# Pooled attention and a four-expert MLP on one core: a batch's keys in two loads, attention pieces at other places of the product loop, and weight sums earlier

## The chip, the cores and the metric

The kernel runs on one core of a Trainium2 chip. The metric is the device time of one execution in microseconds (us). Six executions of the kernel before took 502.47 to 507.32 us, the median is 502.71 us. A core has five engines with a queue of instructions each: TensorE (PE, matrix products), VectorE (DVE), ScalarE (ACT), GpSimd (POOL) and SyncE (SP). Every queue is worked off in order. Semaphores tie the queues together. Transfers are issued from GpSimd's and SP's queues here, and some from ScalarE's at the end.

## The reference

Attention with pooled keys and values over 8 batches of 8 heads (576 tokens, 64 elements a head), and then four experts, weighted by normalised domain probabilities, over all 4608 tokens:

```
k_p = k.reshape(B, H, 72, 8, 64).mean(axis=3)      # 8 rows of keys become one
v_p = v.reshape(B, H, 72, 8, 64).mean(axis=3)
attn = softmax(q @ k_p^T / 8)                       # 576 x 72 for each head
x = (attn @ v_p), heads side by side                # 4608 x 512
p = domain_probs / (domain_probs.sum(-1) + 1e-9)
for e in range(4):
    out += p[:, e] * (relu(x @ w1[e]) @ w2[e])      # 512 -> 1024 -> 512
```

## The kernel before, in words

**Chunks.** The tokens are worked off in nine chunks of 512. Chunk b, for b from 0 to 7, holds the first 512 tokens of batch b. The 64 tokens that each batch leaves over (the remainder) make chunk 8. For each chunk and each expert there is an up product (x times w1, then relu, into `H`) and a down product (`H` times w2, times the probability, added into `acc`).

**Seven products instead of eight.** From chunk 1 on, every up and every down product is split into 2 by 2 blocks, and seven block products of sums and differences take the place of eight (Strassen's scheme in Winograd's form). The sums need VectorE: `weight_sums` and `first_weight_sums` make them once for each expert's w2 and w1 (three into `wt_bf` or `wu_bf`, a fourth in place into the weights, 0.68 to 0.69 us each), `hidden_sums` makes four for each chunk and expert (`S3`, `S2`, two in `H`), `x_sum` four for each chunk (three into `xs`, one in place into `xT`).

**The product loop.** The loop over `g` runs through 7 times 32 steps, and one more. A turn of it is called a slot here; slot g has step i = g mod 7 of chunk-and-expert pair t = g div 7. Chunk c fills slots 28(c-1) to 28(c-1)+27. A slot issues, in this order: a hidden sum (steps 0, 2, 3), the up product's step for one half of the hidden units (unit 0: 4 matmuls), the up step one slot behind for unit 1 (4 matmuls), a hidden sum (step 1), the down product's step one slot behind of the pair before (8 matmuls), then the attention pieces of this slot and the weight sums of this slot. ScalarE takes the steps 0, 1, 2, 3 and 5 of an up product out of PSUM, VectorE the steps 4 and 6 (`relu_sum`, L533). Step 6 and the copy of step 0 (ScalarE, L565) use the same bank: the copy of the next pair waits for the `relu_sum` before, and the next step 1 of TensorE for the copy. VectorE adds the down products into `acc` (L695), except that for expert 0 ScalarE writes the first of each place (L693), and that one step in seven is taken out by ScalarE into `addend` and added by GpSimd (L634, the pooled add). When a chunk's last expert is done, `store` writes `acc` out from SP's queue, and the next chunk's first write of that place waits for the store.

**Attention.** Pieces for a batch: `load_part` (keys and values in four loads of two rows of the eight, the second to fourth adding in the transfer onto the first), `load_q`, `load_q_rem`; `fold_keys` and `fold_values` (VectorE adds the two rows that are left: two `kp` of 0.41 us, one `vp` of 0.41); `queries`, `keys` and `turn` (transposes, from batch 2 on by transfers from SP's queue: `qT`, `kpT`, `xT`); `scores` for each of four pairs of heads (TensorE, then exp on ScalarE, 1.02 us); `context` for each of four rows of tokens (TensorE, then a reciprocal of 0.20 us and a division of 0.69 us on VectorE, `x_tok`); then the four `x_sum`. Every second batch also has the remainder of two batches: `rem_queries`, `rem_scores`, `rem_context`, `rem_turn`. From batch 2 on scores and contexts use one pair of PSUM banks, `att`. Batches 0 and 1 are folded from eight whole rows (`load_whole`, into the room of `wt_bf`) and transposed on TensorE; batch 0 stands ahead of everything, batch 1 in `first_chunk`, which works chunk 0.

**What sets the order.** All five engines are under a manual schedule: each engine's instructions stand in the order in which the Python code emits them. `pieces_later` is a table, written by hand, from slots to attention pieces; the attention of batch b (2 to 7) is put into the slots of chunk b-1, and a few of its pieces sooner. `sums` maps slots to weight sums. Loads from GpSimd's queue stand in the same queue as the pooled adds.

**The places that the change touches.** `load_part` (L113 to L120), the weight sums in `first_chunk` (L730, L746) and in the dictionary `sums` (L874), the table in `pieces_later` (L796 to L829), and the loads of batch 2 ahead of `first_chunk`:

```
        load_w2(3)
        load_part(2, 0)
        load_part(2, 1)
        load_q(2)
        load_part(2, 2)
```

## Time and profile before

| What | before |
|---|---|
| median of six executions | 502.71 us |
| lowest, highest | 502.47, 507.32 us |
| the profiled execution | 507.32 us |
| its span | 505.5 us |
| mean granted TensorE clock | 0.986 |
| busy: TensorE, VectorE, ScalarE, GpSimd | 98%, 74%, 60%, 24% |
| start of slot 0 of the product loop | 76.62 us |
| start of slots 28, 56, 84, 112, 140, 168, 196, 224 | 130.31, 182.74, 236.37, 288.99, 342.12, 393.80, 443.64, 492.55 us |

The profile is of one execution, the slowest of the six. Times in it count from the start of its span. A window's line gives, for a stretch of time, its length, the busy time of each engine with the number of its instructions, the granted clock, the mean share of the 16 transfer engines and the rate. A timeline's line gives start, duration, engine, line of the kernel, operation, output and input; in brackets stands how long the engine had been idle before it, and what ended that idle time. A group that follows without a break is put together on one line (x8). Starts of slots are the starts of the first matmul of the up step of unit 0, found by counting matmuls.

### The profile page before, as it was taken

The numbers are of one execution on the slowest core, as the hardware profiler recorded it, in microseconds if no ns is written. First come the engines' busy times: TensorE is split into PE (matmuls) and PEld (weight loads), VectorE is DVE, ScalarE is ACT, GpSimd is POOL, SyncE is SP. The second block draws the span as 40 slices with busy tenths as digits, with TensorE's granted clock in tenths as the row PEclk, the third lists the DMA queues.
The fourth block names the chain that finished last, engine by engine and source line by source line (L and its number), as shares of the span: only waits on it lengthen the run. The fifth ranks groups of instructions, "written<-read, shape, count | busy, mean of one in ns | idle before, by whom it ended". The sixth has DMA issues, their size and how long they took to land.

```text
span 505.5 us, 11342 instructions
## 1 busy us (share of the span) xinstructions
PE 494.1 (98%) x4613; PEld 410.8 (81%) x4622; DVE 372.2 (74%) x741; ACT 302.3 (60%) x561; POOL 119.3 (24%) x113
## 2 busy tenths in 40 slices
PE   7999999999999999999999999999999999999996
PEld 4766558878888987988788878888888888888885
DVE  3363779989866897778677868887688757876774
ACT  3366624775568557655766576656855576556650
POOL 7230062423344235102441145001101110111010
PEclk9599999999999999999999999999999999999999
DMA  9999999698669849921798179730210010004003
GB/s 161 212 209 203 198 82 112 106 91 66 85 107 98 86 65 111 132 54 21 72 152 80 25 71 134 66 66 22 84 34 1 22 64 1 12 23 84 1 0 84
DMA packets 104611, 41.70 MB, mean 82 GB/s; under 512 B 77664, under 2 KB 103008, under 8 KB 104560
## 3 DMA queue, kind: packets, MB, share of 16 engines
q0 software_dynamic: 60256, 22.69, 42.2%
q1 hardware_dynamic: 43728, 17.77, 18.6%
q8 instruction: 36, 0.59, 0.5%
q10 hardware_dynamic: 576, 0.52, 0.3%
q14 instruction: 15, 0.12, 0.1%
HBM read 45.69 MB, written 9.44 MB: 109 GB/s over the span
## 4 chain that ended last, share of the span: by engine, by line
PE 82%; DVE 8%; DMA 5%; issue 2%; ACT 2%; POOL 0%; DVEq 0%; ACTq 0%; POOLq 0%
PE o_ps L620 34%; PE unit L552 33%; PE unit L479 5%; DVE acc L695 3%; DMA xT<-x_tok 2%; PE o_ps L646 2%; PE att L311 1%; DMA q_sb<-in_q_dram 1%; DMA out_dram<-acc 1%; PE unit L678 1%; DVE H L533 1%; PE att L337 1%; DVE S L189 1%; PE unit L242 1%; DVE x_tok L326 1%
## 5 line engine op out<-in xcount | busy, mean ns | idle before, releaser
L695 DVE SCALAR_TENSOR_TENSOR acc<-o_ps,p_all,acc 128x256 f32<-128x256 f32 (+1 forms) x285 | 127.0, 486 | 59.8 <-PE o_ps L620 40.2
L620 PEld LDWEIGHTS <-H 128*128 128x128 bf16 x1320 | 129.1, 98 | 17.0 <-issue 1.2
L552 PEld LDWEIGHTS <-w_bf 128*128 128x128 bf16 x1024 | 98.0, 98 | 15.7 <-issue 4.2
L533 DVE CUSTOM_DVE_ANT_0 H<-unit,partial 128x512 bf16<-128x512 f32 x128 | 87.6, 686 | 24.4 <-PE unit L552 16.1
L620 PE MATMUL o_ps<-w_bf,H 128*128 128x256 bf16 x792 | 102.6, 273 | 0.4 <-ACT o_ps L628 0.2
L552 PE MATMUL unit<-xT,w_bf 128*128 128x256 bf16 x672 | 96.3, 273 | 0.9 <-ACT unit L565 0.9
L634 POOL TENSOR_TENSOR acc<-acc,addend 128x512 f32<-128x512 f32 x24 | 32.5, 1354 | 274.3 <-ACT addend L632 240.2
L567 ACT COPY partial<-unit 128x512 f32<-128x512 f32 x128 | 72.0, 590 | 33.5 <-PE unit L552 32.9
L552 PEld LDWEIGHTS <-wu_bf 128*128 128x128 bf16 x768 | 73.1, 98 | 10.7 <-issue 2.3
L552 PE MATMUL unit<-xs,wu_bf 128*128 128x256 bf16 x512 | 76.9, 273 | 0.0
L620 PE MATMUL o_ps<-wt_bf,H 128*128 128x256 bf16 x528 | 68.4, 273 | 0.0
L620 PEld LDWEIGHTS <-S 128*128 128x128 bf16 x528 | 51.6, 98 | 7.4 <-issue 1.0
L569 ACT ACTIVATE H<-unit 128x512 bf16<-128x512 f32 x64 | 38.8, 606 | 28.0 <-PE unit L552 28.0
L573 ACT ACTIVATE H<-unit 128x512 bf16<-128x512 f32 x64 | 38.1, 596 | 26.2 <-PE unit L552 25.8
L565 ACT COPY unit<-unit 128x512 f32<-128x512 f32 x64 | 37.3, 583 | 24.4 <-PE unit L552 19.8
L118 POOL DMA_DIRECT2D kraw<-in_k_dram x18 | 25.2, 1398 | 58.4 <-DMA kraw<-in_k_dram 58.4
L552 PE MATMUL unit<-xs,w_bf 128*128 128x256 bf16 x256 | 38.5, 273 | 0.0
L693 ACT ACTIVATE acc<-o_ps,p_all 128x256 f32<-128x256 f32 x72 | 30.2, 471 | 13.6 <-PE o_ps L620 10.6
L620 PE MATMUL o_ps<-w_bf,S 128*128 128x256 bf16 x264 | 34.2, 273 | 0.6 <-DVE acc L695 0.4
L620 PE MATMUL o_ps<-wt_bf,S 128*128 128x256 bf16 x264 | 34.2, 273 | 0.0
L552 PE MATMUL unit<-xT,wu_bf 128*128 128x256 bf16 x224 | 33.7, 273 | 0.0
L315 ACT ACTIVATE expT<-att 72x1024 bf16<-72x1024 f32 x26 | 26.5, 1020 | 7.1 <-PE att L311 7.1
(129 smaller groups left out, 523.7 us busy)
## 6 DMA issues: line engine op xcount, KB each, us to landing
out_dram<-acc SPq DMA_DIRECT2D x32, 256.0 KB, 3.4
w_bf<-in_moe_w_dram POOLq DMA_DIRECT2D x7, 1024.0 KB, 23.4
q_sb<-in_q_dram POOLq DMA_DIRECT2D x7, 512.0 KB, 10.8
kraw<-in_k_dram POOLq DMA_DIRECT2D x24, 144.0 KB, 5.6
vraw<-in_v_dram POOLq DMA_DIRECT2D x24, 144.0 KB, 6.7
w_bf<-in_moe_w_dram POOLq DMA_DIRECT2D x2, 512.0 KB, 11.8
wt_bf<-in_k_dram POOLq DMA_DIRECT2D x2, 288.0 KB, 5.5
wt_bf<-in_v_dram POOLq DMA_DIRECT2D x2, 288.0 KB, 8.8
```

The source lines that it names most:

```text
L315: nc.scalar.activation(out=expT[:, 2 * pair:2 * pair + 2].rearrange("j h a b t -> j b (h a) t"), in_=sc_ps[0:SP].rearrange("j b h (a t) -> ...
L479: nc.tensor.matmul(out_ps, lhsT=w1_bf[:, e, kc, fc * P:(fc + 1) * P], rhs=xT[:, kc, at], start=(kc == 0), stop=(kc == KC - 1), skip_group_ ...
L533: nc.vector._custom_dve(TENSOR_ADD_SAT, out=dst, in0=ps, in1=part, s0=LARGEST, s1=0.0)
L552: nc.tensor.matmul(ps[:, n * HN:(n + 1) * HN], lhsT=lhs[:, kc, f:f + P], rhs=rhs[:, kc, :], start=(not grows and n == 0 and kc == 0), stop ...
L565: nc.scalar.copy(out=units[unit][1][:], in_=ps)
L567: nc.scalar.copy(out=part[:, step - 2], in_=ps)
L569: nc.scalar.activation(out=quarter(0, 0), in_=ps, func=ACT.Relu)
L573: nc.scalar.activation(out=quarter(0, 1), in_=ps, func=ACT.Relu)
L620: nc.tensor.matmul(ps[:, j], lhsT=lhs[:, i, j * P:(j + 1) * P], rhs=rhs[:, i, :], start=(not grows and i == 0 and j == 0), stop=(i == HF - 1),
L634: nc.gpsimd.tensor_add(out=dst, in0=dst, in1=addend[:])
L693: nc.scalar.activation(out=dst, in_=o_ps, func=ACT.Copy, scale=prob)
L695: nc.vector.scalar_tensor_tensor(out=dst, in0=o_ps, scalar=prob, in1=dst, op0=ALU.mult, op1=ALU.add,)
```

## The change

It has four parts.

1. Batch 2's keys: rows 0 to 5 of each eight are loaded in one transfer into the room of expert 2's `wt_bf`, rows 6 and 7 in another into `raw_k`. No key transfer of this batch adds any more; VectorE adds the pieces, `fold_wide(0)` in slot 1 (two adds of 72x1024), `fold_wide(1)` in slot 5 (one). Keys and values now have loads of their own. All loads of batch 2 move from before `first_chunk` to a place inside it, behind `fold_values(1)`.
2. The first three w1 sums of expert 2 move from slots 3, 5 and 6 into the second pass of the first chunk; those of expert 3 from slots 9, 9 and 10 to behind `keys(1)`. The fourth sums go to slots 7 and 13 (from 9 and 13). The last w2 sum of expert 1 goes from slot 9 to slot 8.
3. The pieces of batches 2 to 7 get other slots. Batch 2: keys folded in slot 5 (from 9), values in 12 (from 10), scores in 11, 12, 15, 17 (from 13 to 16), contexts in 18, 19, 21, 22 (from 17, 18, 20, 21), x sums in 25, 26, 26, 26 (from 24, 25, 25, 26). Others: queries and keys six slots ahead of the chunk, scores at -1, 3, 5, 6, contexts at 8, 11, 14, 18, x sums at 21, 22, 25, 26.
4. The loads of the following batch stand at other slots; the queries' load is in the second slot of a chunk from batch 4 on (from the eighteenth).

The arithmetic is the same but for the order of batch 2's key additions. The diff:

```diff
-    def load_part(b, part):
-        for src, raw in ((k, raw_k), (v, raw_v)):
-            rows = src[b].rearrange("h (j r) d -> j h r d", r=POOL)[:, :, 2 * part:2 * part + 2, :]
-            if part:
-                nc.gpsimd.dma_start(out=raw[:], in_=rows, accum_op=ALU.add)
-            else:
-                nc.gpsimd.dma_start(out=raw[:], in_=rows)
+    def rows_of(src, b, lo, hi):
+        return src[b].rearrange("h (j r) d -> j h r d", r=POOL)[:, :, lo:hi, :]
+
+    def load_part(b, what, part):
+        src, raw = ((k, raw_k), (v, raw_v))[what]
+        nc.gpsimd.dma_start(out=raw[:], in_=rows_of(src, b, 2 * part, 2 * part + 2),
+                            accum_op=ALU.add if part else ALU.bypass)
+
+    wide_k = wt_bf[0:SP, 2].rearrange("j s i d -> j (s i d)").rearrange(
+        "j (h r d) -> j h r d", h=H, r=POOL - 2)
+
+    def load_wide(part):
+        if part == 0:
+            nc.gpsimd.dma_start(out=wide_k, in_=rows_of(k, BUSY, 0, POOL - 2))
+        else:
+            nc.gpsimd.dma_start(out=raw_k[:], in_=rows_of(k, BUSY, POOL - 2, POOL))
...
+    def fold_wide(part):
+        a, b, c = (wide_k[:, :, 2 * i:2 * i + 2, :] for i in range(3))
+        if part == 0:
+            nc.vector.tensor_add(out=a, in0=a, in1=b)
+            nc.vector.tensor_add(out=a, in0=a, in1=c)
+        else:
+            nc.vector.tensor_add(out=raw_k[:], in0=raw_k[:], in1=a)
...
-        sums = {e: first_weight_sums(e) for e in range(2)}
+        sums = {e: first_weight_sums(e) for e in range(E)}
...
                     sums[1][i - 4]()
+                    if i < 7:
+                        sums[2][i - 4]()
...
         keys(1, every)
+        each(*sums[3][0:3])
...
         fold_values(1, every)
+        load_wide(0)
+        load_q(2)
+        load_wide(1)
+        load_part(2, 1, 0)
+        load_q_rem(0)
+        load_q_rem(1)
+        for part in range(1, NR):
+            load_part(2, 1, part)
         down_plain(0, 1, 0)
...
-        for b in range(2, B + 1):
-            start = 7 * E * (b - 2)
+        usual = dict(
+            queries=-6, keys=-6, values=-2, scores=(-1, 3, 5, 6), contexts=(8, 11, 14, 18),
+            q=1, k=(-2, 0, 3, 6), v=(-2, 0, 3, 6), x=(21, 22, 25, 26), rem=(-3, 17, 21, 22),
+        )
+        plans = {b: usual for b in range(BUSY, B + 1)}
+        plans[BUSY] = dict(
+            queries=1, keys=5, values=12, scores=(11, 12, 15, 17), contexts=(18, 19, 21, 22),
+            q=9, k=(7, 10, 13, 16), v=(13, 16, 24, 27), x=(25, 26, 26, 26), rem=(2, 6, 8, 9),
+        )
+        plans[B] = dict(usual, x=(25, 25, 26, 26))
+        plans[BUSY + 1] = dict(usual, values=4, v=(5, 8, 11, 14))
...
+            if b == BUSY:
+                put(start + 1, lambda: fold_wide(0))
+                put(start + 5, lambda: load_q_rem(BUSY), lambda: fold_wide(1))
             if b < B:
-                q_at, k_at, scores_at, contexts_at, loads_at = (
-                    (1, 9, (13, 14, 15, 16), (17, 18, 20, 21), (11, 12, 14, 25, 28)) if b == 2
-                    else (0, 3, (10, 11, 12, 13), (15, 16, 18, 20), (5, 6, 8, 11, 14)) if b == 3
-                    else (-4, -4, (3, 4, 5, 6), (8, 9, 11, 13), (-2, 17, 0, 3, 6)))
...
-                put(start + (6 if b == 2 else -3), lambda i=i: rem_queries(i))
-                put(start + (10 if b == 2 else 16), lambda i=i: rem_scores(i))
-                put(start + (12 if b == 2 else 18), lambda i=i: rem_context(i))
-                put(start + (13 if b == 2 else 19), lambda i=i: rem_turn(i))
-            for n, slot in enumerate((24, 25, 25, 26) if b == 2 else (24, 24, 25, 26) if b == 3
-                                     else (16, 16, 20, 23) if b < B
-                                     else (23, 24, 24, 25)):
-                put(start + slot, lambda b=b, n=n: x_sum(b, n))
...
-        load_part(2, 0)
-        load_part(2, 1)
-        load_q(2)
-        load_part(2, 2)
-        load_q_rem(0)
-        load_q_rem(1)
         first_chunk()
...
-        for at, pieces in (((4, 2), weight_sums(3)[2:]), ((3, 5, 6, 9), first_weight_sums(2)), ((9,), weight_sums(1)[3:]), ((14, 14, 16, 16), weight_sums(2)),
-                           ((9, 9, 10, 13), first_weight_sums(3))):
+        for at, pieces in (((4, 2), weight_sums(3)[2:]), ((7,), first_weight_sums(2)[3:]), ((8,), weight_sums(1)[3:]), ((14, 14, 16, 16), weight_sums(2)),
+                           ((13,), first_weight_sums(3)[3:])):
```

## The prediction

> **What bounds the kernel now.** I read the page first: TensorE is busy 98% of the span, so time is won only where TensorE waits. Then I cut the product loop into its chunks of 28 slots (a slot is one turn of the loop, 16 matmuls of 128x256) by windows; the edges are the starts of slots 0, 28, 56 and so on in the timeline.
>
> ```profile
> core 0: us, PE busy (x) PEld busy (x) DVE busy (x) ACT busy (x) POOL busy (x), PEclk, DMA share, GB/s
> 76.62:130.31 53.69, 53.34 (x524) 45.10 (x524) 48.59 (x98) 34.05 (x63) 15.84 (x14) 1.00 0.92 97
> 130.31:182.74 52.43, 51.99 (x498) 44.99 (x496) 41.42 (x86) 33.47 (x62) 18.11 (x16) 1.00 0.77 88
> 182.74:236.37 53.63, 53.08 (x531) 45.43 (x528) 42.96 (x85) 34.52 (x63) 15.41 (x14) 1.00 0.68 81
> 236.37:288.99 52.62, 52.00 (x498) 44.98 (x496) 40.33 (x81) 33.32 (x62) 15.38 (x14) 1.00 0.75 81
> 288.99:342.12 53.13, 52.93 (x530) 45.45 (x528) 42.71 (x83) 34.42 (x63) 15.42 (x14) 1.00 0.73 80
> 342.12:393.80 51.68, 51.68 (x498) 44.98 (x496) 39.36 (x78) 33.53 (x62) 3.81 (x4) 1.00 0.13 35
> 443.64:492.55 48.91, 48.91 (x451) 43.82 (x449) 34.62 (x66) 29.63 (x58) 4.54 (x5) 1.00 0.12 28
> ```
>
> The granted clock is 1.00 in all of them. The last line has no attention: 28 slots in 48.91, so 1.75 a slot. The sixth holds one batch's attention and no wait: 2.77 more, which is four score pieces of 0.43 and four context pieces of 0.26. The remainder pieces of every second batch add 0.90 (slot 72 with scores, slot 74 with context), and slot 0 has 0.41 of the plain product. So chunks 1 to 5 should take 52.99, 51.68, 52.58, 51.68 and 52.58. They take 0.70, 0.75, 1.05, 0.94 and 0.55 more: 3.99 us is all that the loop can give back. The timeline says who is late:
>
> ```profile
> 113.81 0.42 PE L337 MATMUL att<-vp,expT 72*128 72x65 bf16 x8 [0.20 <-DVE x_tok L326]
> ...
> 127.45 0.43 DVE L189 TENSOR_TENSOR xs<-xT 128x512 bf16<-128x512 bf16 x1 [1.30 <-DMA xT<-x_tok]
> ...
> 131.28 0.68 DVE L533 CUSTOM_DVE_ANT_0 H<-unit,partial 128x512 bf16<-128x512 f32 x1
> 132.04 0.57 ACT L565 COPY unit<-unit 128x512 f32<-128x512 f32 x1 [1.80 <-DVE H L533]
> 132.66 0.70 PE L552 MATMUL unit<-xT,w_bf 128*128 128x256 bf16 x5 [0.44 <-ACT unit L565]
> ...
> 185.08 0.38 PE L552 MATMUL unit<-xT,w_bf 128*128 128x256 bf16 x2 [0.43 <-ACT unit L565]
> ...
> 260.25 0.84 ACT L693 ACTIVATE acc<-o_ps,p_all 128x256 f32<-128x256 f32 x2 [2.38 <-DMA out_dram<-acc]
> ...
> 303.50 2.50 DVE L189 TENSOR_TENSOR S<-H 128x1024 bf16<-128x1024 bf16 x1
> 303.61 1.83 POOL L634 TENSOR_TENSOR acc<-acc,addend 128x512 f32<-128x512 f32 x1
> ```
>
> In chunk 1 VectorE's queue is late (slot 9 loses 0.24, 16 loses 0.09, 18 loses 0.40: slot lengths against 1.75 plus their pieces). At slots 28 and 30 (0.75) VectorE first waits 1.30 for the last transpose of x; so `relu_sum` ends at 131.95, ScalarE's copy (L565) waits for it, and TensorE for the copy. Slots 56 and 58 (0.74) show the same chain behind crowded slots 52 to 54. Slot 72 loses 0.28 to ScalarE's copy L628. Slot 96 loses 0.42 to a store that lands late, 103 loses 0.52 to a transposed x that lands 1.43 late, and 121 loses 0.53 where a VectorE sum stands still beside GpSimd's add.
>
> **The change, part by part.** Every number below is of the profiled execution: 507.32, its span 505.5 and 1.8 around it. It is 4.61 above the median of the six, 502.71. I take the loop's waits to be alike in the others and put the sum on the median.
>
> *Weight sums sooner.* Six of 0.69 leave slots 3, 5, 6, 9, 9 and 10. Slots 7 to 10 held 2.32, 0.68, 4.25 and 1.78 of VectorE work (4.25 is `H` 0.69, two `kp` of 0.41, `w1_bf` and `w2_bf` 0.68 each, two `wu_bf` of 0.69) in 7.86 of TensorE; now they hold 3.00, 2.26, 0.69 and 0.68. Three sums go into the second pass of the first chunk. Two fall in idle stretches of 2 to 3 us. The third follows the sum at 50.76 to 51.44 and ends at 52.04 (operations overlap by 0.09), where the next add started at 51.62. The queue then has no gap up to the `qT` copies, so these start 0.32 later, at 55.98 and 56.31; TensorE, which wrote the two banks again at 56.20 and 56.45, waits: cost 0.32 (ends 0, if the 0.6 of other work shifts, and 0.6, the whole sum). The other three stand after the `kpT` copy, before an idle of 2.92 (60.76 to 63.68); fold of values ends near 62.6. They cost nothing; were that cover gone, 1.9.
>
> *Keys of batch 2.* GpSimd's four key loads become two, and two accumulating issues of 1.39 go. VectorE gets three adds of about 0.69 (the fold of 72x1024 took 0.686): two in slot 1, one in slot 5. Counting from slot 0, S2 ends at 80.96, the two adds at 82.2; slot 1's list is late by 0.6, slot 3 lost 0.69, so the queue is level by slot 4. Cost 0. All loads of batch 2 now stand on GpSimd's queue behind the fold of batch 1's values, at about 63. Before, the second part was issued at 64.92, so only bytes of the first parts come later. In the transfers between 60 and 130 us a 512 KB `q_sb` took 8.8 to land and the 144 KB parts 6.1 and 6.8, so the six rows (432 KB by size) should land before 72; VectorE wants them at 80.9. The four value parts wait for each other: issued near 66, 74, 80 and 86, the last issue ends near 88; GpSimd's pooled add of slot 5 wants to start at 89. Cost 0, ends 0 and 0.53 (the price of 121, if the chain is later). On SP's queue `qTr` moves to slot 2, `kpT` to 6, `x_rem` to 9, each behind stores; their inputs are there and their readers stand four slots or more behind: 0.
>
> *Attention of batch 2.* Contexts at 18, 19, 21, 22. Chunk 1's 0.70 goes. I added VectorE's queue slot by slot, each operation at the later of its input and its predecessor's end; by this sum the division of slot 17 ends 2.01 after the start of slot 18 before (the trace: 113.76, 2.06). After, the division of slot 21 ends 1.85 into slot 22, TensorE wants the bank at 1.75: 0.15 back. On SP's queue the transpose of batch 3's queries (issue 3.21 at 123.87) is now ahead of x's last transpose, and keys' transpose behind both. From slot 22: division 1.85, first x transpose 1.2, `qT` 2.0 to 3.2, x 2.4 to 5 from issue to landing (113.82 to 116.19, 122.33 to 127.30): 7.7 to 11. The sum that reads x comes at 8.2; five queue entries (2.6) later `relu_sum` must be done 0.65 before slot 29, at 12.3: nothing is lost up to a landing at 9.7. Keys land at 9.1 to 12, scores of slot 27 want them at 10.8. I take 0.2, ends 0 and 1.3, for the 0.75 that goes.
>
> *Later batches.* Scores, contexts and x sums stand further apart; slots 52 to 54 drop from 6.88 to 5.22 of VectorE work, and x's last transposition has 4.7 us before its reader with queries' load already over. So 0.74 (56, 58) and 0.52 (103) go. The heaviest new slot, 77, holds 3.63 in 2.23; by the same queue sum adds end at most 1.46 after a slot's end, and the banks allow 1.95. Cost 0.
>
> *What it leaves.* 96 and 121 have one root: GpSimd's pooled add stands in its queue behind a value part (L118) which waits for the part before; the add starts 2.1 to 3.5 after the slot. After the change the order there is the same, with the query load put in front. ScalarE's 72 has the same list. I count half of 0.42, 0.53 and 0.28 as gone: 0.62 (ends 0 and 1.23).
>
> The rows for that are `S` 2.50 against 0.68 and the add's 1.83 against 1.27. [...]
>
> Sum: gone 0.70 + 0.75 + 0.74 + 0.52 + 0.62 = 3.33; new 0.32 + 0.15 + 0.2 + 0.1 = 0.77. Net 2.56: 502.71 - 2.56 = **500.1**.
>
> **Rivals.** *A: all waits go.* 3.99 less the 0.32 that is sure: 499.0. For it: no queue sum passes its limit. Against: GpSimd's order at the late adds stays. *B: the waits move.* The three half-terms stay (0.62 back) and SP's order at slot 22 costs 1.0 instead of 0.2: 500.1 + 1.4 = 501.5. For it: the transposes at 119.51 and 122.33 landed 6.2 and 5.0 later with key and value parts in flight. Against: only one part is in flight there. *C: the six rows come late.* In-order VectorE stands at slot 1 until they land. L109 loads took 23.6 and 21.9 to land at 20 to 50 us, behind weights: 63.1 + 23.6 = 86.7, against 82.3 (80.96 and 1.3 of slack): 4.4 lost, 504.5, slower than before; it decides from a landing at 84.9 on. Against: weights have landed by then, since the first part landed by 64.9.
>
> **How the numbers follow.** Forecast 0.51, A 0.18, B 0.24, C 0.07. About 0.5% (2.5 us) is what a measurement here tells from no change, so 500.2 is the border and the forecast lies on it: 0.6 of the forecast, all of A and little of B are faster, 0.50 in all; slower than 505.2 is the far part of C and what I don't see, 0.06; 0.44 between. Range: A's bound and 0.3 below, B with the upper ends of its terms above: 498.7 to 502.2; C and half of the unseen lie outside.
>
> **What would show it.** Right: chunks near 53.1, 51.9, 52.7, 52.0, 52.9; no wait of `xs` on `xT` at slots 25 and 105; TensorE idle 0.3 before the `qT` transposes at 56. Wrong: VectorE idle before L213-like adds of 72x1024 at slot 1, TensorE waiting on `kpT` in slot 27, GpSimd's add of slot 5 past 91, or stores that hold ScalarE at the first expert of each chunk.

## The result, and the profile after

The changed kernel is slower. Its median is 508.27 us over 32 executions (503.16 to 514.15), that of the kernel before 503.16 us over 69 on the same chips. The ratio is 1.0072, with a 95% interval of 1.0053 to 1.0091; it is taken over the undisturbed executions alone, the medians over all. The forecast was 500.1, with a range that ended at 502.2.

The two profiled executions, 509.63 us (span 507.8) and 507.32, can't be compared by their totals. The one before had 13.7 us at half clock (a granted clock of 0.50) ahead of the loop and started slot 0 at 76.62; the one after started it at 72.67. A measure that leaves this out is the time from the start of slot 0 to the start of slot 196: 367.02 us before, 373.27 after, 6.25 more. It is called the loop's length below.

The windows of the changed kernel, cut at slots 0, 28, 56 and so on as before (columns: from:to, length, busy time and instructions of TensorE, its weight loads, VectorE, ScalarE and GpSimd, granted clock, share of the transfer engines, GB/s):

```profile
72.67:134.14 61.47, 56.42 (x529) 46.10 (x528) 50.34 (x100) 34.98 (x63) 17.94 (x16) 0.94 0.81 85
134.14:185.81 51.67, 51.67 (x498) 44.99 (x496) 40.52 (x83) 33.50 (x62) 16.85 (x15) 1.00 0.69 85
185.81:239.48 53.67, 52.93 (x530) 45.43 (x529) 43.18 (x84) 34.47 (x63) 15.54 (x14) 1.00 0.61 79
239.48:292.24 52.76, 52.01 (x499) 44.99 (x497) 42.40 (x82) 33.48 (x62) 15.50 (x14) 1.00 0.65 81
292.24:344.84 52.60, 52.60 (x530) 45.47 (x529) 41.84 (x84) 34.35 (x63) 15.55 (x14) 1.00 0.63 81
344.84:396.10 51.26, 51.26 (x494) 44.96 (x493) 39.24 (x78) 33.50 (x62) 3.39 (x4) 1.00 0.13 35
```

The forecast named 53.1, 51.9, 52.7, 52.0 and 52.9 for the first five. Chunks 2 and 5 are there, chunks 3 and 4 are 1.0 and 0.8 over, and chunk 1 is 8.4 over, with a granted clock of 0.94. Of the 8.4, 0.43 is no loss: the new table puts the first score piece of batch 3 into slot 27, and the forecast had not moved it. (Chunk 6 is shorter by as much, 51.26 instead of 51.68.) TensorE's timeline shows where in chunk 1 (start, duration, engine, line, operation, in brackets the idle time before it and what ended it):

```profile
94.94 1.04 PE L638 MATMUL o_ps<-wt_bf,H 128*128 128x256 bf16 x8
100.27 0.61 PE L329 MATMUL att<-qT,kpT 64*128 64x256 bf16 x4 [4.29 <-DMA kpT<-kp]
...
102.49 1.92 PE L638 MATMUL o_ps<-w_bf,S 128*128 128x256 bf16 x8
104.33 0.61 PE L329 MATMUL att<-qT,kpT 64*128 64x256 bf16 x4
```

Before the first scores of batch 2, in slot 11, TensorE waits 4.29 us for the transpose of the keys. Behind it, eight matmuls that took 1.04 take 1.92: the clock has fallen. Three windows around it:

```profile
97.00:100.00 3.00, 0.00 (x0) 0.00 (x0) 0.00 (x0) 0.00 (x0) 0.00 (x0) 0.83 0.90 130
100.00:103.00 3.00, 2.73 (x15) 1.72 (x16) 0.17 (x1) 1.56 (x2) 0.00 (x0) 0.50 1.62 111
103.00:106.00 3.00, 3.00 (x18) 1.67 (x17) 1.79 (x5) 1.02 (x1) 1.40 (x1) 0.53 0.03 2
```

In the first no engine works at all, and the clock falls in it, at 98.96; in the next two it is 0.50 and 0.53. In all 6.8 us were at half clock, by which slots 12 and 13 lost 1.89 and 0.44. (The loss of a slot is its length less 1.75 and less the time of its attention pieces. The expectations below have some numbers that are up to 0.05 higher.) What the wait was for: the same transpose, from issue to landing, in the kernel before and in the changed kernel.

```profile
95.05 1.21 SPq L229 DMA_TRANSPOSE kpT<-kp  x1
102.76 0.39 PE L311 MATMUL att<-qT,kpT 64*128 64x256 bf16 x4
DMA to landing us min/median/max: 4.6/4.6/4.6
```

```profile
DMA to landing us min/median/max: 11.4/11.4/11.4
```

Before, nobody on TensorE waited for it: it landed at 99.66 and was read by the scores at 102.76. After, it was issued at 88.86 and landed at 100.22. Since the two loops start 3.95 apart, the times are better counted from the start of slot 0: it was issued 2.2 sooner (16.2 instead of 18.4) and landed 4.5 later (27.6 instead of 23.0), while its first reader stood 2.8 sooner (ready at 95.97, so 23.3 instead of 26.1). SP's queue and GpSimd's queue of the changed kernel at that time:

```profile
86.43 2.38 SPq L721 DMA_DIRECT2D out_dram<-acc  x2
88.86 1.25 SPq L247 DMA_TRANSPOSE kpT<-kp  x1
90.43 0.38 SPq L721 DMA_DIRECT2D out_dram<-acc  x1
92.47 1.67 SPq L418 DMA_TRANSPOSE x_rem<-x_tok  x1
```

```profile
84.68 1.72 POOL L652 TENSOR_TENSOR acc<-acc,addend 128x512 f32<-128x512 f32 x1
85.95 1.11 POOL L154 DMA_DIRECT2D q_rem<-in_q_dram  x1
87.33 0.86 POOL L119 DMA_DIRECT2D kraw<-in_k_dram  x1 [0.28 <-DVE kp L241]
88.18 0.92 POOL L139 DMA_DIRECT2D q_sb<-in_q_dram  x1
89.07 0.71 POOL L154 DMA_DIRECT2D q_rem<-in_q_dram  x1
```

Two stores of 256 KB stand ahead of the transpose on its own queue, and the 512 KB load of batch 3's queries (`q_sb`) is issued 0.7 ahead of it on the other. The stores also hold up the issue. The pooled keys were done at 87.03, but the second store was issued only at 88.44, when VectorE's add into `acc` had ended (88.42), and the transpose behind it. In the kernel before it was issued at once when the pooled keys were done (95.02).

The other three losses are of one kind, a VectorE sum beside GpSimd's pooled add. VectorE at the two `kp` sums and at slot 65, with the add of slot 65:

```profile
84.90 2.13 DVE L241 TENSOR_TENSOR kp<-kraw 72x512 bf16<-72x512 bf16 x2
...
199.91 3.03 DVE L199 TENSOR_TENSOR S<-H 128x1024 bf16<-128x1024 bf16 x1
200.56 1.82 POOL L652 TENSOR_TENSOR acc<-acc,addend 128x512 f32<-128x512 f32 x1
```

The two `kp` sums take 2.13 instead of 0.8 and cost 0.85 in slot 7 (84.68 to 86.40 is the add). `S` takes 3.03 instead of 0.68 and costs 1.06 in slot 65; slot 93 loses 1.07 the same way.

So the loop's losses are 4.57 in slot 11, 2.33 in slots 12 and 13, 0.85, 1.06 and 1.07 by the sums, and 0.30 in slots 16 and 22: some 10.2, against the 3.99 that it lost before. The difference, 6.2, is that of the loop's lengths.

### The profile page after: what moved, and what is told of

Its sections match the earlier page's. It is cut to its first block, busy times and chain, and to the rows that moved or that the text cites. A ratio compares the mean times of both kernels' runs of the same rounds, so it can differ in the third digit from the quotient of the medians.

```text
span 507.8 us, 11350 instructions
## 1 busy us (share of the span) xinstructions
PE 492.0 (97%) x4613; PEld 408.1 (80%) x4622; DVE 378.4 (75%) x744; ACT 303.3 (60%) x561; POOL 115.9 (23%) x111
## 4 chain that ended last, share of the span: by engine, by line
PE 85%; DVE 8%; DMA 4%; issue 1%; ACT 0%; POOL 0%; SPq 0%; DVEq 0%; ACTq 0%; POOLq 0%
PE o_ps L638 37%; PE unit L570 36%; PE unit L497 4%; DVE acc L713 2%; DMA kpT<-kp 2%; DMA wt_bf<-in_v_dram 2%; PE att L329 2%; DVE S L199 1%; PE o_ps L664 1%; PE att L355 1%; PE unit L696 1%; DVE wt_bf L199 1%; DVE kp L241 1%; DVE H L551 1%; DVE x_tok L344 0%
## 5 line engine op out<-in xcount | busy, mean ns | idle before, releaser
L551 DVE CUSTOM_DVE_ANT_0 H<-unit,partial 128x512 bf16<-128x512 f32 x128 | 87.8, 686 | 31.1 <-PE unit L570 26.1
L587 ACT ACTIVATE H<-unit 128x512 bf16<-128x512 f32 x64 | 38.7, 605 | 27.3 <-PE unit L570 27.3
L119 POOL DMA_DIRECT2D vraw<-in_v_dram x24 | 31.6, 1315 | 36.3 <-DMA vraw<-in_v_dram 24.3
```

What stands on the lines that cost most here:

```text
L119: nc.gpsimd.dma_start(out=raw[:], in_=rows_of(src, b, 2 * part, 2 * part + 2), accum_op=ALU.add if part else ALU.bypass)
L551: nc.vector._custom_dve(TENSOR_ADD_SAT, out=dst, in0=ps, in1=part, s0=LARGEST, s1=0.0)
L587: nc.scalar.activation(out=quarter(0, 0), in_=ps, func=ACT.Relu)
```

## The experiments

Each is a short edit of the changed kernel unless it is said otherwise. The loop's length stands beside the median where it tells more. A trace is of one execution, and the executions of a kernel differ by several us, so a wait is read from the trace and the whole time from the median.

### The query load later (e1)

```diff
-            q=9, k=(7, 10, 13, 16), v=(13, 16, 24, 27),
+            q=14, k=(7, 10, 13, 16), v=(13, 16, 24, 27),
```

> The changed kernel with one number altered: the load of batch 3's queries stands at slot 14 of the loop instead of slot 9, behind all key loads and the first value load of batch 3 on GpSimd's queue. Theory T1 (the 512 KB query load, which GpSimd issued at 88.18 us, 0.7 us ahead of the transpose of batch 2's keys, shares the transfers' bandwidth with it and so stretches it from 2.6-4.4 to 11.1 us): the keys' transpose lands within 5 us of its issue, TensorE's wait of 4.29 before the first scores of slot 11 falls to 0-0.5, the stretch at half clock behind it goes too, and the time falls by 6 to 7 us against the changed kernel, to about 501.5. Rival T2 (the transpose is slow because of the place to which the change moved it, among the stores of the slots 6 to 8 and the key load, whatever the queries do): it still takes over 8 us, TensorE waits over 2, and the time stays within 2 us of the changed kernel's.

Measured: median 504.01, ratio to before 0.9983 (0.9944 to 1.0022); loop 368.32. The transpose took 7.7 us, between what the two theories said:

```profile
98.56 0.39 PE L329 MATMUL att<-qT,kpT 64*128 64x256 bf16 x4 [1.55 <-DMA kpT<-kp]
```

The wait falls to 1.55 and the clock stays at 1.00 from 96 to 106. So the query load is a part of it, not all. Other losses stood in this execution: a wait of 0.58 for the remainder's queries in slot 6, 0.52 in slot 9, 0.60 in slot 27, 0.39 in slots 28 and 30, and 1.10 in slot 93 for an `S` beside the pooled add.

### Work for TensorE while it would wait (e2)

```diff
+        if b == BUSY and pair == 0:
+            for _ in range(20):
+                open_bank(bank[:, 0])
```

> The changed kernel with 20 matmuls of 128x512 added ahead of the first scores of batch 2 (slot 11). They write the bank that the scores then write again, so nothing of their result is used: they only keep TensorE at work while it would wait for the keys' transpose. By the matmuls of 128x256 (1.75 us for 16) 20 of them take about 4.4 us, as long as the wait of 4.29. Theory T3 (the half clock from about 99 to 106 us is a consequence of that wait): the granted clock stays 1.00 through slots 11 to 13, and the time is about 2.4 us less than the changed kernel's although work was added (slots 12 and 13 lost 1.93 and 0.48). Rival T4 (the half clock comes of something else, as the work done before): the clock falls all the same and the time is equal to the changed kernel's or up to 4.4 more.

Measured: median 506.73, ratio 1.0052 (1.0013 to 1.0090), 1.5 under the changed kernel's median where 2.4 were expected. In the profiled execution the transpose took 8.5 and landed at 97.62, so the wait would have been 2.2 only (TensorE's other work was done at 95.45); TensorE was busy throughout and the clock stayed at 1.00. By itself this does not settle what the half clock comes of. The holds below do.

### The pooled add ahead of the value load (e3)

```diff
-            q=1, k=(-2, 0, 3, 6), v=(-2, 0, 3, 6),
+            q=1, k=(-2, 0, 5, 8), v=(-2, 0, 5, 8),
```

> The changed kernel with the third key and value loads of batches 5 to 8 at slot 5 instead of 3 of their chunks, and the fourth at 8 instead of 6, so that on GpSimd's queue the pooled add of each chunk stands ahead of the third value load, which waits for the second to land. Theory T5 (slots 65 and 93 lose 1.10 each because the add is late and so runs beside VectorE's S sum, which grows from 0.68 to 3.03): the S sums of slots 65 and 93 take about 0.7, the two losses go, and the time falls by about 2.2 us against the changed kernel. Rival T6 (the add would meet another VectorE sum wherever it stands, or the later parts make the keys of those batches late): the time stays within 0.7 us, and another operation with two inputs takes over 1.5 beside the add.

Measured: median 507.48, ratio 1.0049 (1.0007 to 1.0091); loop 370.76, 2.5 shorter than the changed kernel's. GpSimd's add and VectorE's `S` of slot 65:

```profile
197.14 1.26 POOL L652 TENSOR_TENSOR acc<-acc,addend 128x512 f32<-128x512 f32 x1 [3.23 <-ACT addend L650]
198.36 1.41 POOL L119 DMA_DIRECT2D kraw<-in_k_dram  x1
```

```profile
199.08 0.68 DVE L199 TENSOR_TENSOR S<-H 128x1024 bf16<-128x1024 bf16 x1
```

The add stands ahead of the load, is over before `S`, and both have their plain lengths; slots 65 and 93 lose nothing. T5 holds in the trace, and not by chance: with this edit the three adds of slots 62, 90 and 118 all take 1.26, while in the traces of the changed kernel, of e1, e2 and e4 the adds of these places take 1.82 to 1.84, in the changed kernel beside hidden sums of 3.03, 3.04 and 1.58. The third of these sums is not the first of a pair's (`S` from `H`) but the second (`S` from `H` and `S`), and TensorE does not wait in that chunk (52.60 busy of 52.60). The median can't tell it, since the wait of slot 11 (4.46 here) and the half clock behind it are still there, and the executions of this kernel differ by several us (502.31 to 513.82).

### The last key rows sooner (e4)

```diff
-                put(start + 5, lambda: load_q_rem(BUSY), lambda: fold_wide(1))
+                put(start + 3, lambda: fold_wide(1))
+                put(start + 5, lambda: load_q_rem(BUSY))
```

> The changed kernel with the last add of batch 2's wide key rows at slot 3 instead of 5, so that the pooled keys of batch 2 are summed before GpSimd's pooled add of chunk 1 begins. Theory T7 (slot 7 loses 0.89 because the sum of the pooled keys took 1.80 beside that add): the sums take about 0.4 each, slot 7 is level, and the time falls by about 0.9 us; the keys' transpose is issued no earlier than its slot, so the wait of slot 11 stays at 3 to 4.5. Rival (the time that the queue gains at slot 7 only makes the wait at slot 11 longer, since that ends with the transpose, whatever comes before): no change of the whole, with the wait 0.9 longer.

Measured: median 506.94, ratio 1.0029 (0.9986 to 1.0073). The two `kp` sums:

```profile
84.64 0.75 DVE L241 TENSOR_TENSOR kp<-kraw 72x512 bf16<-72x512 bf16 x2
```

Slot 7 is level, as T7 said, but the edit is not what did it: the add began at 86.51 here, 1.8 later than in the changed kernel and after the `kp` sums, which stand where they stood. In e1 and e2, without this edit, the add was as late and slot 7 as level. So T7 is not tested by this run; e7 and e8, where the sums come two slots sooner and end ahead of the add, are what supports it. The add ran beside an `S` of 2.22 at 86.69, which held nobody up. In slot 6 TensorE waited 0.72 for the transpose of the remainder's queries, as it did for some time in e1 and e2. The wait of slot 11 was 1.94, less than expected (no fall of the clock followed): GpSimd's queue was 1.8 later here (the remainder's load at 87.72 instead of 85.95), so that the key part was still under way, and the query load behind it, when the store ahead of the transpose had landed. The table in the next section has these times.

### The keys ahead of the stores (e7)

```diff
-            queries=1, keys=5, values=12,
+            queries=1, keys=3, values=12,
```

with `fold_wide(1)` in slot 3 as above.

> The changed kernel with the keys of batch 2 two slots sooner: the last add of its wide rows and the two sums of the pooled keys at slot 3 instead of 5, so that the transpose stands at slot 4 of SP's queue, ahead of the stores of slots 5 and 6 instead of behind them. The query load of batch 3 stays at slot 9. Theory T8 (stores and transposes on SP's queue land in the order of their issue: 90.07, 92.83, 100.22, 101.90, 102.58 in the changed kernel; so the transpose first waits for the store in front of it, 4.0 us, and then shares its time with the query load of GpSimd's queue, 7.4 us): the transpose is issued near 83 and lands by 88, TensorE does not wait for it at slot 11, no half clock follows, and the time falls by 6 to 7 us, to about 501.5. Rival T9 (VectorE, with 1.5 us of sums more in slot 4, is late with the hidden sums and TensorE loses it there): the wait of slot 11 goes, but slots 5 and 6 lose 0.5 to 1.5 us, and the time is 502.5 or more.

Measured: median 502.68, ratio 0.9974 (0.9935 to 1.0013), 5.6 under the changed kernel; loop 364.70, 8.6 shorter than it. The transpose:

```profile
DMA to landing us min/median/max: 5.0/5.0/5.0
```

No wait in slot 11, no half clock in the loop; slot 5 loses 0.17, so T9's price is small. The query load stood where the change put it. What it loses besides is above all `S` in slot 65 (1.11). The median is 1.2 above the 501.5 expected, and the ratio does not tell the kernel from the one before; against the changed kernel the gain is clear.

### Three corrections together (e8)

The last edit, the query load at 14, and the loads at 5 and 8.

> The changed kernel with three corrections together: the keys of batch 2 two slots sooner as in e7, the query load of batch 3 at slot 14 instead of 9 as in e1, and the third and fourth key and value loads of batches 5 to 8 at slots 5 and 8 as in e3. If the causes are those named so far, the three are worth the wait of 4.29, the half clock of 2.4, the 0.89 of slot 7 and the twice 1.10 of slots 65 and 93: 9.8 us less than the changed kernel's profiled execution, and about 499 to 500 as a median, below both kernels. Rival: other waits take their place (the transposes and loads of batch 3 come closer to their readers with the queries at slot 14), and the time stays at 501.5 to 503.

Measured: median 501.37, ratio 0.9959 (0.9923 to 0.9995): faster than the kernel before. The transpose took 2.7 us. The windows, cut as above:

```profile
72.30:126.21 53.91, 53.82 (x529) 45.05 (x528) 48.43 (x98) 34.61 (x63) 17.89 (x16) 1.00 0.76 95
126.21:178.37 52.16, 51.99 (x499) 45.02 (x497) 41.92 (x85) 33.68 (x62) 16.93 (x15) 1.00 0.70 84
178.37:230.98 52.61, 52.61 (x531) 45.46 (x529) 41.09 (x84) 34.49 (x63) 15.46 (x14) 1.00 0.64 81
230.98:282.66 51.68, 51.68 (x499) 44.97 (x497) 40.28 (x82) 33.51 (x62) 15.42 (x14) 1.00 0.66 82
282.66:335.27 52.61, 52.61 (x531) 45.48 (x529) 41.09 (x84) 34.49 (x63) 15.45 (x14) 1.00 0.65 81
```

TensorE is busy in all of these five chunks but 0.26 us. The loop takes 364.06, 9.2 less than the changed kernel's. The median is 1.4 over the 499 to 500 expected; six of its twelve executions took 499.2 to 501.3, and the others, up to 505.8, have no profile.

### The scores later (e9)

```diff
-            scores=(11, 12, 15, 17),
+            scores=(13, 14, 15, 17),
```

> The changed kernel with the first two score pieces of batch 2 at slots 13 and 14 instead of 11 and 12, so that 3.5 us more of products stand before the first reader of the keys' transpose; loads, stores and transposes stay as they are. Theory T8 with T3: the transpose still takes 8 to 11.4 us, TensorE waits 0 to 0.9 for it at slot 13, and since no long wait is left, the clock stays at 1.00; the time falls by 5.5 to 7 us against the changed kernel. Rival T4 (the half clock has another cause than the wait): it still falls to half near 99 to 106 us, and the time falls by only 3.5 to 4.3.

Measured: median 506.60, ratio 1.0025 (0.9992 to 1.0058), only 1.7 under the changed kernel. In the profiled execution the transpose took 10.7 and TensorE lost 0.2 for it, with the transfers as crowded as in the changed kernel and the clock at full:

```profile
97.00:104.00 7.00, 6.86 (x65) 5.38 (x63) 5.52 (x11) 4.26 (x10) 0.00 (x0) 1.00 1.64 127
131.70:135.10 3.40, 3.40 (x19) 2.42 (x17) 3.40 (x9) 1.32 (x2) 1.61 (x3) 0.50 0.93 75
```

So in slots 11 to 13 T8 and T3 are right. The second line is a wait that was not expected: the transpose of batch 3's keys came 2.04 late in slot 27, behind a transpose of batch 3's queries that took 8.9 beside a value part, and a stretch at half clock followed that. That wait accounts for a part of the missed time; what the other executions lost is not on record.

### The query load early in the kernel before (e6)

```diff
-                put(start + q_too, lambda b=b: load_q(b + 1), ...)
+                put(start + (9 if b == 2 else q_too), lambda b=b: load_q(b + 1), ...)
```

> The kernel before with one number altered: the load of batch 3's queries at slot 9 instead of 12, ahead of the key and value part of slot 11 on GpSimd's queue, so that it is in flight when the transpose of batch 2's keys is issued (95.05). Theory T8: the transpose, 4.6 us before, takes 7 to 11 and lands at 102 to 106; its first reader stood at 102.76, so TensorE waits 0 to 3 us there, and the time grows by 0 to 3 us, more where a wait is long enough to halve the clock. Rival: the query load is harmless there, the transpose takes 4 to 5 us, and the time is the same within 0.5.

Measured: median 510.62, ratio 1.0082 (1.0043 to 1.0122): one load (with its remainder) moved by three slots costs as much as the whole change did. The transpose of batch 2's keys took 8.6 us, as expected, but it was not the first to be late:

```profile
97.34 0.41 PE L374 MATMUL att<-qTr,kpT 64*128 64x64 bf16 x16 [3.21 <-DMA qTr<-q_rem]
```

```profile
97.70:101.10 3.40, 3.40 (x21) 2.40 (x18) 0.69 (x1) 1.61 (x2) 0.00 (x0) 0.50 1.86 142
```

The transpose of the remainder's queries, ahead of it on SP's queue, took 8.5 instead of 3.7 (counted from the landing of the store ahead of it, 3.4 instead of 0.5); TensorE waited for that in slot 10, and 3.4 us at half clock followed. The keys' transpose was then hidden behind the delay. T8's mechanism holds, at one reader earlier than it was said.

### Batch 2's attention back at its old slots (e12 and e13)

```diff
-            queries=1, keys=5, values=12, scores=(11, 12, 15, 17), contexts=(18, 19, 21, 22),
-            q=9, k=(7, 10, 13, 16), v=(13, 16, 24, 27), x=(25, 26, 26, 26), rem=(2, 6, 8, 9),
+            queries=1, keys=9, values=10, scores=(13, 14, 15, 16), contexts=(17, 18, 20, 21),
+            q=12, k=(11, 14, 25, 28), v=(11, 14, 25, 28), x=(24, 25, 25, 26), rem=(6, 10, 12, 13),
```

> The changed kernel with the attention and loads of batch 2's chunk put back to the slots of the kernel before (keys 9, scores 13 to 16, contexts 17 to 21, queries of batch 3 at 12, key and value parts at 11, 14, 25 and 28, remainder at 6 to 13); the wide key rows, the sooner weight sums and the spread of the later batches stay as changed. Theory T8: the keys' transpose stands again behind one store and ahead of the query load, lands 3 us before its reader, no long wait and no half clock arise in the loop; what the old slots cost (0.70 in chunk 1 and 0.75 at slots 28 and 30, less what the sooner sums and wide rows mend) comes back, and so do the late sums of slots 65 and 93 as they are in the changed kernel: 5 to 7 us less than the changed kernel, near 502. Rival T10 (the wide rows or the sooner sums are what costs, not the place of the keys): the time stays above 505, with waits in slots 0 to 12.

Measured: median 507.91, ratio 1.0081 (1.0042 to 1.0121), where 502 was expected. The put-back was flawed: two key parts of batch 3 now stood behind the sum that reads them, so its keys were pooled from half of their rows. In slots 0 to 13 the loop was level and the transpose of batch 2's keys took 4.7, against T10. Most of the loss, 5.3 of some 6.7, is in slots 27 and 28, where a key and a value part, issued at 119.41 and 120.26, ran beside the transpose of batch 3's keys:

```profile
129.53 0.61 PE L329 MATMUL att<-qT,kpT 64*128 64x256 bf16 x4 [3.71 <-DMA kpT<-kp]
```

It took 8.6 to land, and 3.4 us at half clock followed. (Another 0.84 in slot 37 and 0.67 in slot 93 are an `S` beside the pooled add.) The mended form has the key parts at 11, 13, 15, 17 and the value parts at 13, 16, 24, 27:

> The repaired form of e12: batch 2's attention (keys 9, scores 13 to 16, contexts 17 to 21, remainder 6 to 13) and the query load of batch 3 (12) again at the slots of the kernel before, the rest as in the changed kernel; but the parts of batch 3's keys at 11, 13, 15 and 17 and of its values at 13, 16, 24 and 27, so that all key parts are issued ahead of the pooled keys of slot 22 (in e12 two were left behind it, so that the keys of batch 3 were summed from half of their rows, and a key and a value part stood beside the transpose of batch 3's keys). Theory T8: no wait for the keys' transpose at slot 13 nor at slot 27, no half clock in the loop; what is left is the 0.3 to 0.7 of slots 16 to 18 and what slots 65 and 93 lose: a loop some 7 us shorter than the changed kernel's, and a median of 501.5 to 503. Rival T10 (something else in the change costs the 5 us): over 505. Rival T11 (the transpose of batch 3's keys is late wherever batch 3's loads stand): a wait of 1 us or more at slot 27 remains, and the time is 503 to 506.

Measured: median 500.98, ratio 0.9953 (0.9929 to 0.9977), with executions from 499.48 to 502.29: faster than the kernel before, and the narrowest spread of all. The loop takes 365.20. No wait at slots 13 and 27, the clock at 1.00 in every chunk:

```profile
72.11:125.98 53.87, 53.60 (x529) 45.15 (x528) 48.91 (x100) 34.00 (x63) 18.10 (x16) 1.00 0.86 98
125.98:177.66 51.68, 51.68 (x499) 45.00 (x497) 40.54 (x83) 33.51 (x62) 16.84 (x15) 1.00 0.69 85
177.66:230.95 53.29, 52.93 (x530) 45.46 (x529) 42.80 (x84) 34.48 (x63) 15.53 (x14) 1.00 0.63 80
```

What is left is 0.1 and 0.35 in slots 16 and 18, and `S` beside the late add in slots 65 and 93 (0.68 and 0.90). T10 and T11 fall. All other parts of the change are in this kernel: they are worth 2.4 us by the ratio. What turned them into a loss is in the slots of batch 2's attention and of the loads beside it, which this run puts back together; e1, e6 and e7 single out the place of the keys and of batch 3's query load.

### Holding TensorE on purpose (e10 and e11)

In the kernel before, five times in the last two chunks:

```diff
+            if g in hold:
+                open_bank(att[:, 0])
+                nc.scalar.copy(out=held[:], in_=att[:, 0, 0:NT // 2])
+                for _ in range(hold[g]):
+                    nc.gpsimd.tensor_add(out=held[:], in0=held[:], in1=held[:])
+                nc.tensor.matmul(att[:, 1], lhsT=ident[:], rhs=held[:].bitcast(BF16)[:, 0:NT], ...)
```

> The kernel before with TensorE held five times on purpose, in the two last chunks, which have no attention: at slots 174, 184, 194, 204 and 213 it waits for a ScalarE copy and 2, 4, 6, 8 and 12 GpSimd sums of 128x256, whose result is not used (the added work has nothing to do with the output). By the row of the 128x512 sum (1.27) a sum of 128x256 is estimated at 0.65, and the waits at about 2.2, 3.5, 4.8, 6.1 and 8.7 us. Theory T3 (a long wait of TensorE is followed by a stretch at half clock): the granted clock is 0.5 for some us after the longer waits, and not after the shortest; the length from which it starts lies above 2.1 (no fall after the 2.11 of e4, a fall of 3.4 us after the 2.21 of e9). Rival T4 (the clock falls for another reason, as the crowd of transfers, of which there is none here): 1.00 after all five.

> As e10, with 1, 3, 5, 3 and 5 sums at the same five slots: waits estimated at 1.6, 2.9, 4.1, 2.9 and 4.1 us. Theory T3: no fall of the clock after the first; a fall after both of 4.1, as after the 4.29 of the changed kernel, of the same 6.8 us; after those of 2.9 a shorter fall of about 3.4 or none, which places the border. Rival T4: 1.00 after all five.

Measured: 542.70 and 531.45 us, one execution each. The waits of the first kernel, and then of the second:

```profile
403.36 0.49 PE L906 MATMUL att<-held,ident 128*128 128x512 bf16 x1 [2.17 <-POOL held L905]
...
454.07 0.58 PE L906 MATMUL att<-held,ident 128*128 128x512 bf16 x1 [6.18 <-POOL held L905]
...
507.90 0.58 PE L906 MATMUL att<-held,ident 128*128 128x512 bf16 x1 [8.79 <-POOL held L905]
```

```profile
402.12 0.38 PE L906 MATMUL att<-held,ident 128*128 128x512 bf16 x1 [1.15 <-POOL held L905]
424.37 0.59 PE L906 MATMUL att<-held,ident 128*128 128x512 bf16 x1 [2.58 <-POOL held L905]
...
474.66 0.58 PE L906 MATMUL att<-held,ident 128*128 128x512 bf16 x1 [2.80 <-POOL held L905]
496.23 0.59 PE L906 MATMUL att<-held,ident 128*128 128x512 bf16 x1 [3.96 <-POOL held L905]
```

Windows of the second kernel at its first, second and fourth hold:

```profile
403.00:407.00 4.00, 4.00 (x39) 3.59 (x37) 2.77 (x5) 2.60 (x6) 0.00 (x0) 1.00 0.39 135
...
422.70:429.60 6.90, 5.23 (x24) 3.60 (x24) 1.11 (x3) 1.17 (x2) 1.46 (x3) 0.51 0.01 2
...
473.90:477.40 3.50, 2.74 (x13) 1.76 (x13) 0.00 (x0) 0.94 (x2) 1.37 (x3) 0.51 0.43 50
```

The clock falls in or behind nine of the ten holds, with little in transfer (shares of 0.00 to 0.43 in the windows of the holds). T3 holds and T4 falls. (The waits that the first expectation names as 2.11 and 2.21 are 1.94 and 2.04 by the rows of e4 and e9.) How long it falls goes roughly by the wait: the last section has the table.

## Why the prediction was wrong, point by point

- **The step that failed** is the one on SP's queue: `kpT` moves to slot 6, "behind stores; their inputs are there and their readers stand four slots or more behind: 0." It looked at the inputs and counted slots up to the reader, and gave the transfer no price. And the load of batch 3's queries, moved from slot 12 to slot 9, was given none at all. The issue, too, came later than that: 5.3 after the start of slot 6 (83.56), in slot 8, since the pooled keys were done at 87.03 and the stores ahead on the queue held it for 1.8 more; three slots were left up to the reader. Together this cost the wait of 4.29. The list of what would make the prediction wrong had TensorE waiting on `kpT` in slot 27, of the next batch, not in slot 11. The rows to price it with had been read: an x transpose of 2.4 to 5, a `q_sb` of 8.8, and in rival B transposes that landed 6.2 and 5.0 later beside key and value parts. They were used for batch 3's queue at slot 22 and not for batch 2's at slot 6.
- **What the runs showed in its place** is in this table, of times at which the transfers landed. Where the query load ran beside it all the time, the transpose needed 6.5 to 7.7 from the landing of the transfer ahead of it, and else 1.2 to 4.1.

| kernel | `kpT` issued | transfer ahead on SP's queue landed | `kpT` landed | from the one to the other | on GpSimd's queue in that time |
|---|---|---|---|---|---|
| before | 95.05 | 95.61 | 99.66 | 4.0 | key part |
| changed | 88.86 | 92.83 | 100.22 | 7.4 | query load |
| add ahead (e3) | 88.29 | 92.09 | 99.82 | 7.7 | query load |
| scores later (e9) | 90.22 | 94.38 | 100.92 | 6.5 | query load |
| key rows sooner (e4) | 89.37 | 93.75 | 97.66 | 3.9 | key part to 96.56, then query load |
| query load later (e1) | 90.85 | 95.38 | 98.52 | 3.1 | remainder, key part |
| keys sooner (e7) | 88.30 | 89.29 | 93.25 | 4.0 | value part |
| three corrections (e8) | 82.74 | 84.21 | 85.45 | 1.2 | value part, issued at 83.31 |
| work for TensorE (e2) | 89.16 | 93.81 | 97.62 | 3.8 | key part to 96.48, then query load |
| before, query load early (e6) | 92.55 | 98.80 | 101.14 | 2.3 | key part (query load to 98.62) |
| old slots (e12) | 91.00 | 91.67 | 95.66 | 4.0 | key part |
| old slots mended (e13) | 91.17 | 92.14 | 96.25 | 4.1 | key part, query load behind it |

- **The half clock** (2.3 us in slots 12 and 13) was in no rival. The trace of before has no wait in the loop long enough to show it: the longest is the 0.44 for ScalarE's copy.
- **The pooled add beside VectorE's sums** was seen, and mis-sized. The forecast's sum has 0.1 for slot 5, where the two `kp` sums meet the add. No run shows that term: in the changed kernel these sums took 2.13 instead of 0.8 and cost 0.85, in slot 7. The half-terms of slots 96, 121 and 72 were counted as 0.62 gained: all 1.23 of them went, but two new ones of 1.06 and 1.07 came in slots 65 and 93, so the term is 0.9 lost. The price of slot 121 (0.53, for an `S` of 2.50) was taken as the upper end though it was one case; the runs showed an `S` of 2.16 (e2) to 3.04 (slot 93 of the changed kernel) beside the add.
- **What was right.** The waits of chunk 1 (0.70) went but for 0.11 in slot 16; slots 28, 30, 56 and 58 (0.75 and 0.74) and slot 103 (0.52) lose nothing, and no `xs` waits at slots 25 and 105. The weight sum in the first chunk cost 0.34 around the `qT` transposes (0.32 forecast): from the first of them to the matmuls behind the `kpT` transposes passed 3.25 instead of 2.91. TensorE lost 0.19 in slot 22 (0.15 forecast). SP's order at slot 22, put at 0.2, cost 0 in the profiled execution of the changed kernel; the trace of e9, in which these pieces stand at the same slots, has 2.1 there, past the upper end of 1.3. The 0 is in part luck, then. The six rows landed at 67.04, against rival C.
- **The sum.** The forecast had the loop lose 1.1 (3.99, less 3.33, plus 0.45 of new waits); the loop of the three corrections is 2.96 shorter than that of before, where 2.88 was forecast. That they agree is in part luck: e8 loses 0.5 in slots 28 and 30, where 0.2 was forecast, and nothing in slots 72, 96 and 121, where 0.61 was. In the sum the other parts were priced well, but for the waits that these corrections take away.

## What to carry to other kernels

When a transfer is moved to an earlier place, price its landing and not its issue: list what stands ahead of it on its own queue and what the other queue has in flight at the new place, and take the nearest row for that company (here, from the landing of the transfer ahead of it, 1.2 to 4.1 without the 512 KB load beside it all the time and 6.5 to 7.7 with it). Add what the queue ahead of it still waits for (1.8 here). Leave its reader at least that far behind, or put the small transfer that TensorE waits for ahead of the bulk ones. And count a TensorE wait of over 2 us not at its length alone: the half clock cost another 1.6 us (e6, where the slot from 97.69 to 101.07 took 3.38 instead of 1.75) to 2.3 us (the changed kernel) in the slots behind it here.

## What the runs showed of the hardware that was not expected

**The clock after a wait.** TensorE's longest waits in the loops of the runs, and the length of the stretch with a granted clock of 0.50 that the trace records for each. The longer ones begin while the wait still lasts (in the changed kernel at 98.96, 1.3 before its end):

| wait, us | 1.15 | 1.55 | 1.94 | 2.04 | 2.17 | 2.58 | 2.80 | 3.21 | 3.27 | 3.71 | 3.96 | 4.29 | 4.46 | 5.49 | 6.18 | 6.25 | 8.79 |
|---|---|---|---|---|---|---|---|---|---|---|---|---|---|---|---|---|---|
| half clock, us | 0 | 0 | 0 | 3.4 | 3.4 | 6.8 | 3.4 | 3.4 | 3.4 | 3.4 | 6.8 | 6.8 | 6.8 | 6.8 | 6.8 | 6.8 | 10.2 |
| run | e11 | e1 | e4 | e9 | e10 | e11 | e11 | e6 | e10 | e12 | e11 | changed | e3 | e11 | e10 | e10 | e10 |

The three waits up to 1.94 were followed by none, and all fourteen from 2.04 on by some: in these runs the border lies near 2.0. The lengths are one, two and three times 3.41 (the changed kernel's is 6.83, and the stretch ahead of the loop of before 13.65, four times). In e10 the stretches begin within 0.3 us behind 403.4, 427.3, 451.2, 478.5 and 502.4, so some 23.9, 23.9, 27.3 and 23.9 apart, which is 7, 7, 8 and 7 times 3.41. The length of the wait does not set that of the stretch alone, since 2.58 was followed by 6.8 and 3.71 by 3.4. What else sets it was not shown.

**Transfers of one queue landed in the order of their issue, and two queues moved packets in the same time.** In the changed kernel SP's landed at 90.07, 92.83, 100.22, 101.90 and 102.58. In the traces of the two kernels no transfer landed ahead of one issued before it by the same engine (81 of SP in each, 83 and 81 of GpSimd, 4 of ScalarE in each). From 92.83 to 100.22, with the transpose and the query load in flight, the queues q0 and q1 of the changed kernel's trace moved 0.44 MB each, in 1217 and 1142 packets. In the table of the transposes one needs 6.5 to 7.7 beside the query load, and 1.2 to 4.1 else. Why the query load slows it more than a key or value part does is not shown.

**Both sums stretch.** Beside each other, `S` took up to 3.04 instead of 0.68 (slot 93 of the changed kernel) and the pooled add 1.82 instead of 1.27. From the start of `S` in slot 65 of the changed kernel to its end passed 3.03 us, longer than `S` and the add one after the other would take (1.95). So the add's length on top of that of the sum is too low a price here.

**Open.** Executions of the changed kernel differ by 11 us, those of the mended one by 2.8. Some of such differences is at half clock ahead of the loop, with 13.7 us of it in the profiled executions of before and of e7 (a mean granted clock of 0.986 in both) and 6.8 in those of e6 and e9 (0.988, with the 3.4 in their loops). What decides that was not tried.
